# Attention and a gated MLP in one kernel, ordered by a written-out plan: groups 2 and 3 of the heads summed singly instead of as a pair, and a new order

## The chip, the cores and the metric

One core of a Trainium2 chip runs the whole program. The metric is the device time of one execution in microseconds (us). The engines are TensorE (PE in the profile, with its weight loads as PEld), VectorE (DVE), ScalarE (ACT), GpSimd (POOL) and SyncE (SP), which here only issues DMAs.

## The reference

There are 8 batches, 12 heads, 448 positions and 64 columns per head. The attention's output, laid out as 448 x 768 per batch, goes into a spatially gated MLP.

```python
q_n, k_n = rmsnorm(q, g_q), rmsnorm(k, g_k)            # over the 64 columns
attn = softmax(q_n @ k_n.T / sqrt(64));  x = attn @ v  # per batch and head
h = maximum(x @ w_in, 0)                               # 768 -> 1024
u, v = h[..., :512], h[..., 512:]
v_n = (v - mean(v)) / sqrt(var(v) + 1e-6)
out = (u * (w_spatial @ v_n + b_spatial)) @ w_out      # 512 -> 768, float32
```

## The kernel before

**Groups.** The 96 heads are 24 groups of four: group G belongs to batch G // 3. For each group, q and k are loaded (`op_L`, L287; i is 0 for q, 1 for k, 2 for v), squared (`op_Q`, on the engine that the plan names), summed over the 64 columns on VectorE (`op_R`), turned into a factor by a small log and exponential on ScalarE (`op_I`, `op_J`) and normalised (`op_N`, VectorE or GpSimd). They are transposed either by seven TensorE products (`op_P`) and a copy out of PSUM (`op_K`), or by a transposing DMA on SP's queue (`op_T`, L482; for k the scaled copy `op_Z` follows). V is cast to bf16 by `op_F`.

**Softmax.** A group has seven score blocks (`op_S`, L501): eight products of 64 rows by 32 columns of the array, each 448 long, into two PSUM banks. For group 0 a block (but the last) uses only the cells of one row half, each twice (`unit`, L494). ScalarE takes the exponential of a block into SBUF (`op_E`, L514, 168 in all). Then each of the seven columns of blocks is multiplied three times: with ones for the sum (`op_s`), and with the two halves of V (`op_a`, `op_b`). One such step for one group is here called a pass. It is four products, one per head, and the two heads of a pair lie in different row halves:

```python
for l in range(4):
    r, hh = divmod(l, 2)
    at = 64 * (hh ^ flip(G))
    ...
    pe.matmul(out=ps[32 * l:32 * l + 32, where[kind, G][0], 0:S], lhsT=w, rhs=et_of(G, r, c)[at:at + 64],
              start=(n == 1), stop=(n == C), tile_position=(at, 32 * l))
```

A pass takes four of the eight cells of 64 x 32. `flip` (L309) is 1 for the groups in the set `SECOND`; for those the two heads change row halves, and their V comes in by two loads of half the size, which `op_L` issues. A plan word `a.G.c.1` runs the pass of G and that of G + 1, a paired pass, which takes all eight cells; `a.G.c.0` runs that of G alone, a single pass. Before the change all groups are paired, (0, 1), (2, 3) and so on. `op_D` and `op_d` on ScalarE make the reciprocal of the sum by log and exponential, and `op_X` (L570, VectorE) scales a half of V's result into xt, the input of the MLP; there are two xt tiles, for even and for odd batches.

**MLP.** Per batch: V products (`op_V`, L589) for three row tiles, the fourth with the tail of the previous batch's output in `op_W` (L618), U products (`op_U`, L655), the statistics and normalisation (`op_c`, `op_B`, `op_M`, `op_m`, `op_A`), the spatial products (`op_H`, L669), the gate (`op_G`) and the output products (`op_O`, L683) with their copies and stores. The first of all is batch 0's first V product.

**Order.** All of it is issued in the order of the words in `PLAN`; each engine runs its share strictly in that order, and the framework adds waits for data and buffers. A word is `name.arguments/slots/engine`, with slots as base-36 digits (PSUM banks for S and the passes). Ten buffers hold loaded tiles, three hold squares, four normalised tiles, 22 exponentials. Operations of VectorE and GpSimd between SBUF tiles that share a port (`port`, L280) also wait for the other engine's last such operation. `op_z` (L249) issues idle products of 448 columns on TensorE, whose result is not used.

Of the kernel before, what the change touches and what calls it, by code (L numbers as in the profile page):

```python
# [19 lines left out]
SECOND = {1, 3, 5, 7, 9, 11, 13, 15, 17, 19, 21, 23}  # L20

PLAN = """
l.0.0/0/a l.1.0/1 gl.0//g l.0.1//a l.1.1 L.1.1/2 gl.1//g setup L.1.0/3 L.2.1/4 L.2.0/5 z.12/0 L.3.1/6 q.0.0/0/v
L.3.0/7 q.1.0/1/a r.0.0 wb/0 r.1.0 L.4.0/8 q.0.1//a L.5.0/9 q.1.1//a r.0.1 i.0//a r.1.1 j.0//a n.0.0//g i.1//a j.1//a
gA Q.1.1/2/a ws n.0.1//v p.0.0/0 L.1.2/0 R.1.1 n.1.0//g gB/1 Q.1.0/0/a p.0.1/2 n.1.1//g gC k.0.0/0/a p.1.0/1 R.1.0
Q.2.1/1/g L.4.1/1 k.0.1//a p.1.1/3 k.1.0/0/v I.1//a k.1.1//v S.0.0/01 J.1//a S.0.1/45 Q.2.0/2/a wi.0.1 N.1.1/0/v
S.0.6/23 E.0.1/0/a R.2.0 L.0.2/2 P.1.1/6 N.1.0/1/g E.0.6/1/a S.0.3/45 R.2.1 E.0.0/2/a S.0.2/23 Q.3.0/0/g
L.5.1/3 E.0.3/3/a K.1.1/1/v S.0.5/01 P.1.0/7 I.2//a E.0.2/4/a K.1.0/1/v wi.0.2 J.2//a E.0.5/5/a N.2.1/2/v
S.1.3/23 S.1.6/45 E.1.3/6/a N.2.0/3/v L.7.1/4 P.2.1/0 Q.3.1/2/a S.1.1/67 K.2.1/2/v L.6.0/5 S.1.5/12 Q.5.0/1/g
E.1.6/7/a P.2.0/3 R.3.1 E.1.5/8/a S.1.0/45 Y.0/0 R.3.0 Q.4.0/2/g E.1.1/9/a K.2.0/2/v E.1.0/a/a S.1.4/12 S.0.4/67 R.5.0  # L30
Y.2/3 I.3//a E.1.4/b/a Q.4.1/0/g y.0//v S.1.2/45 J.3//a y.2//v E.0.4/c/a S.2.6/01 S.2.3/23 E.2.6/d/a wx//g N.3.0/0/v
s.0.3.1/67 s.0.6.1 E.1.2/e/a S.2.1/01 F.1//v s.0.4.1 L.3.2/7 s.0.5.1 E.2.3/f/a R.4.0 s.0.2.1 N.3.1/1/g s.0.1.1
S.2.5/45 s.0.0.1 L.9.1/0 E.2.1/g/a P.3.0/2 R.4.1 E.2.5/h/a Q.5.1/1/v L.2.2/6 P.3.1/3 D.0/1/a I.4//a S.2.4/01
K.3.1/3/v Y.1/4 F.0//g E.2.4/i/a K.3.0/3/v J.4//a wi.0.3 L.6.1/2 D.1/0/a S.3.1/56 y.1//v b.0.5.1/01 wi.1.1 S.2.0/23
N.4.0/2/v E.3.1/j/a a.0.6.1/47 b.0.3.1 b.0.1.1 a.0.0.1 d.1//a b.0.0.1 S.3.0/56 L.7.0/8 E.2.0/k/a b.0.6.1 F.3//v
b.0.4.1 b.0.2.1 a.0.2.1 N.4.1/3/v a.0.3.1 L.8.1/7 E.3.0/l/a S.3.6/23 E.3.6/a/a X.1.1 S.3.3/56 Q.6.0/2/g R.5.1 P.4.0/1
d.0//a Y.3/2 K.4.0/0/v I.5//a E.3.3/1/a wi.1.0 P.4.1/3 F.2//v wi.0.0 J.5//a y.3//a N.5.1/0/v S.3.4/56 wi.1.3 a.0.5.1
a.0.4.1 E.3.4/7/a S.3.5/12 wi.1.2 a.0.1.1 K.4.1/0/v Q.6.1/0/g E.3.5/e/a s.2.0.1/56 X.0.1 s.2.4.1 s.2.1.1 s.2.3.1 X.0.0
Q.7.1/1/a s.2.6.1 s.2.5.1 S.2.2/01 S.3.2/23 N.5.0/1/g R.6.1 E.2.2/0/a P.5.1/4 E.3.2/c/a X.1.0 S.4.4/01 K.5.1/1/v
Q.9.1/0/g E.4.4/6/a T.5.0/1 b.2.5.1/72 s.2.2.1 R.6.0 b.2.4.1 a.2.1.1/34 D.2/1/a a.2.3.1 b.2.6.1 a.2.6.1 L.4.2/1 d.2//a  # L40
R.7.1 a.2.4.1 Q.7.0/2/g b.2.3.1 D.3/0/a L.5.2/6 b.2.0.1 S.4.6/01 b.2.1.1 I.6//a b.2.2.1 E.4.6/8/a a.2.0.1 a.2.2.1
X.2.1 L.8.0/3 S.4.1/56 Q.8.1/1/g a.2.5.1 d.3//a L.9.0/9 X.2.0 E.4.1/4/a V.0.0.0/7 X.3.1 V.0.0.1 J.6//a X.3.0 V.0.0.2
N.6.1/2/g R.7.0 S.4.5/56 c.0.0//a S.4.2/01 S.5.5/23 E.4.2/5/a V.0.2.1/4 R.8.1 V.0.1.0/7 N.6.0/3/g L.10.0/2 E.4.5/b/a
# [111 lines left out]
def kernel(  # L155
# [153 lines left out]
    def flip(G):  # L309
        return int(G in SECOND)  # L310

# [440 lines left out]
```

## Time and profile before

| | |
|---|---|
| median of 3 runs | 269.86 us (269.24 to 270.5) |
| the profiled execution | 270.1 us, span 268.3 us, mean granted TensorE clock 0.987 |
| TensorE / ScalarE / VectorE / GpSimd busy | 249.9 / 220.5 / 210.1 / 127.8 us |
| first V product of batch 0 | 46.98 us |
| DMA moved | 55.48 MB, mean 207 GB/s |

Times within the execution are microseconds from the span's start. Busy time is the union of an engine's instructions, and rows of TensorE, ScalarE and VectorE overlap a little because the engines are pipelined. In timeline rows the columns are start, length, engine, line, operation, tiles and count, and in brackets the idle time before with what ended it.

### The profile page before, as it was taken

Reading aid. Unit: us, or ns where it says so; the run is one execution under the profiler, and the core shown is the slowest. Engines: PE = TensorE matmul, PEld = TensorE weight load, DVE = VectorE, ACT = ScalarE, POOL = GpSimd, SP = SyncE. Lnnn points to the kernel's source line nnn. Section 1 sums busy time; section 2 is a strip of 40 time slices with the busy share of each in tenths; the row PEclk is TensorE's granted clock in tenths of the full one; section 3 lists DMA queues with packets and bytes.
Section 4 is the critical chain, followed back from the end, with each engine's and each line's share of the span. In section 5 each row is a group of like instructions: output and inputs, shape, how many; then the busy total and the mean of one; then the engine's idle time right before and its main releaser. Section 6 shows DMA issues by size and latency. Waiting matters only on the chain.

```text
span 268.3 us, 9975 instructions
## 1 busy us (share of the span) xinstructions
PE 249.9 (93%) x4296; PEld 128.0 (48%) x4296; DVE 210.1 (78%) x363; ACT 220.5 (82%) x363; POOL 127.8 (48%) x99
## 2 busy tenths in 40 slices
PE   5788786999999998999999999999999999999993
PEld 2434544445445554445545454454445546645551
DVE  5979998899889886899899989786868554457841
ACT  4999998899989998999989998999798976430532
POOL 2859569995465951656755358840464000000000
PEclk9968999999999999999999999999999999999999
DMA  7999899999999999999997999999374114110225
GB/s 248 366 268 330 237 256 153 313 250 288 189 220 254 323 226 306 283 284 244 199 288 175 259 220 250 308 136 173 131 166 121 61 61 149 74 45 2 88 116 209
DMA packets 58462, 55.48 MB, mean 207 GB/s; under 512 B 34609, under 2 KB 54130, under 8 KB 58418
## 3 DMA queue, kind: packets, MB, share of 16 engines
q1 hardware_dynamic: 56098, 51.52, 75.5%
q0 software_dynamic: 1952, 2.76, 5.8%
q8 instruction: 33, 0.54, 0.8%
q10 hardware_dynamic: 368, 0.56, 0.6%
q14 instruction: 11, 0.09, 0.1%
HBM read 38.55 MB, written 11.01 MB: 185 GB/s over the span
## 4 chain that ended last, share of the span: by engine, by line
PE 75%; DMA 10%; POOL 5%; issue 3%; DVE 2%; ACT 2%; SPq 0%; POOLq 0%; DVEq 0%
PE ps L544 15%; PE ps L655 13%; PE ps L683 11%; PE ps L589 11%; PE ps L509 11%; PE ps L669 8%; DMA raw<-in_k_dram 7%; PE ps L618 5%; POOL nrm L429 3%; DMA kr<-nrm 2%; DMA raw<-in_q_dram 1%; POOL sqt L385 1%; POOL nrm L437 1%; ACT et L517 1%; DVE os L366 1%
## 5 line engine op out<-in xcount | busy, mean ns | idle before, releaser
L517 ACT ACTIVATE et<-ps 128x896 bf16<-128x896 f32 x168 | 146.3, 922 | 11.3 <-PE ps L509 10.0
L429 POOL TENSOR_TENSOR nrm<-raw,rs 128x896 bf16<-128x896 f32 x37 | 62.0, 1687 | 42.0 <-ACT rs L414 34.0
L509 PE MATMUL ps<-qT,kT 64*32 64x448 bf16 x1344 | 57.5, 360 | 6.0 <-ACT et L517 2.0
L396 DVE TENSOR_REDUCE ss<-sqt 128x14 f32<-128x896 f32 x46 | 48.5, 1073 | 1.2 <-POOL sqt L385 1.2
L385 POOL TENSOR_TENSOR sqt<-raw 128x896 f32<-128x896 f32 x24 | 40.1, 1678 | 11.1 <-DVE nrm L429 4.7
L655 PE MATMUL ps<-xt,w_in 128*128 128x448 bf16 x192 | 43.2, 353 | 0.0
L544 PE MATMUL ps<-et,vt 64*32 64x448 bf16 x1344 | 41.5, 349 | 1.8 <-DVE xt L573 1.4
L589 PE MATMUL ps<-w_in,xt 128*128 128x512 bf16 x144 | 37.8, 380 | 0.0
L573 DVE TENSOR_TENSOR xt<-ps,rc 128x448 bf16<-128x448 f32 x48 | 27.7, 617 | 12.0 <-PE ps L544 7.5
L683 PE MATMUL ps<-w_out,gt 128*128 128x384 bf16 x192 | 36.2, 326 | 0.4 <-ACT et L517 0.4
L509 PEld LDWEIGHTS <-kT 64*32 64x32 bf16 x1344 | 20.3, 90 | 30.8 <-issue 21.7
L544 PEld LDWEIGHTS <-vt 64*32 64x32 bf16 x1344 | 21.8, 92 | 12.8 <-issue 3.4
L366 DVE COPY os<-ps 128x384 f32<-128x384 f32 (+1 forms) x32 | 17.5, 554 | 12.6 <-PE ps L683 7.5
L669 PE MATMUL ps<-w_spT,vn 128*128 128x448 bf16 (+1 forms) x128 | 27.3, 353 | 0.0
L655 PEld LDWEIGHTS <-w_in 128*128 128x128 bf16 x192 | 17.6, 98 | 20.1 <-issue 4.8
L683 PEld LDWEIGHTS <-gt 128*128 128x128 bf16 x192 | 17.7, 98 | 16.5 <-issue 4.3
L674 DVE TENSOR_TENSOR gt<-ps,us 128x448 bf16<-128x448 f32 x32 | 19.0, 619 | 7.3 <-PE ps L669 6.0
L544 PE MATMUL ps<-et,ones 64*32 64x448 bf16 x672 | 23.5, 350 | 0.6 <-ACT et L517 0.6
L320 POOL CAST vt<-raw 128x896 bf16<-128x896 f32 x16 | 14.8, 929 | 17.8 <-DVE sqt L385 8.6
L630 DVE BATCH_NORM_STATS2 s<-vs 128x6 f32<-128x512 bf16 (+1 forms) x32 | 21.7, 680 | 1.4 <-ACT vs L580 0.9
L364 ACT ACTIVATE os<-ps 128x384 f32<-128x384 f32 (+1 forms) x32 | 15.6, 490 | 6.2 <-PE ps L683 5.1
L589 PEld LDWEIGHTS <-xt 128*128 128x128 bf16 x144 | 12.7, 98 | 16.7 <-issue 5.2
(65 smaller groups left out, 262.5 us busy)
## 6 DMA issues: line engine op xcount, KB each, us to landing
raw<-in_k_dram SPq DMA_DIRECT2D x23, 448.0 KB, 6.0
raw<-in_q_dram SPq DMA_DIRECT2D x23, 448.0 KB, 6.3
out_dram<-os SPq DMA_DIRECT2D x24, 384.0 KB, 2.4
raw<-in_v_dram SPq DMA_DIRECT2D x24, 224.0 KB, 4.5
raw<-in_v_dram SPq DMA_DIRECT2D x12, 448.0 KB, 4.8
w_in<-in_moe_w_in_dram POOLq DMA_DIRECT2D x8, 192.0 KB, 7.1
out_dram<-os SPq DMA_DIRECT2D x7, 192.0 KB, 3.3
w_out<-in_moe_w_out_dram POOLq DMA_DIRECT2D x1, 768.0 KB, 9.2
```

Source lines behind the costliest of these rows:

```text
L385: port(eng, eng.tensor_tensor(out=t, in0=x, in1=x, op=ALU.mult))
L396: dve.tensor_reduce(out=sss[G % 3][:, i].rearrange("p r c -> p (r c)"), in_=sqt[where.pop(("sq", G, i))].rearrange("p r (c d) -> p (r c) d ...
L429: port(eng, eng.tensor_tensor(out=nrm[sl[0]].rearrange("p c r d -> p r c d"), in0=raw[where["raw", G, i]].rearrange("p r (c d) -> p r c d" ...
L509: pe.matmul(out=ps[at:at + 32, sl[n], 0:S], lhsT=kT[64 * r:64 * r + 64, c, 64 * hh + 32 * x:64 * hh + 32 * x + 32], rhs=qT[64 * r:64 * r + ...
L517: act.activation(out=ets[sl[0]].rearrange("q r (p c) -> q r p c", c=C), in_=ps[:, a:b + 1:b - a, 0:S].rearrange("q r (c p) -> q r p c", c= ...
L544: pe.matmul(out=ps[32 * l:32 * l + 32, where[kind, G][0], 0:S], lhsT=w, rhs=et_of(G, r, c)[at:at + 64], start=(n == 1), stop=(n == C), til ...
L573: dve.tensor_tensor(out=xts[b % 2][:, 2 * g + half, :], in0=ps[:, where.pop(("ab"[half], G))[0], 0:S], in1=rcs[where["rc", G]], op=ALU.mult)
L589: pe.matmul(out=ps[:, bank, :], lhsT=xts[b % 2][:, j, 128 * m:128 * m + 128], rhs=w_in[:, j % 2, j // 2, DH:], start=(n == 1 and j == 2 * ...
L630: dve.bn_stats(out=s6, in_=vss[b % SLOTS["vs"]][rows, m, :])
L655: pe.matmul(out=ps[:, bank, 0:S], lhsT=w_in[:, j % 2, j // 2, 128 * f:128 * f + 128], rhs=xts[b % 2][:, j, :], start=(n == 1 and j == 2 * ...
L669: pe.matmul(out=ps[:, sl[0], 0:S], lhsT=vns[b % SLOTS["vn"]][rows, m, 128 * f:128 * f + 128], rhs=w_spT[rows, m, :], start=(m == 0), stop= ...
L683: pe.matmul(out=ps[:, sl[0], 0:384], lhsT=gts[b % 2][:, f, 128 * m:128 * m + 128], rhs=w_out[:, f, 384 * h:384 * h + 384], start=(f == 0), ...
```

## The change

Group 3 leaves the set of flipped groups, the words of the passes of groups 2 and 3 become single (42 for 21), and the whole order is new: every line of `PLAN` differs. The engines of some words change, the idle products become 22 in four places (`z.11`, `z.5`, `z.4`, `z.2`, and `h.3`, three of 64 columns) instead of 12 in one, and group 1's q is transposed by a DMA (`T.1.0`) instead of by TensorE (`P.1.0`, `K.1.0`). The operations' functions are the same, one line further down.

```diff
-SECOND = {1, 3, 5, 7, 9, 11, 13, 15, 17, 19, 21, 23}
+SECOND = {1, 5, 7, 9, 11, 13, 15, 17, 19, 21, 23}
...
-Q.9.1/0/g E.4.4/6/a T.5.0/1 b.2.5.1/72 s.2.2.1 R.6.0 b.2.4.1 a.2.1.1/34 D.2/1/a a.2.3.1 b.2.6.1 a.2.6.1 L.4.2/1 d.2//a
...
+E.3.0/l/a S.3.1/12 a.2.2.0/0 wi.1.0 Q.7.1/1/v s.2.0.0 E.3.1/6/a b.2.5.0/4 S.3.3/56 wi.0.1 s.2.2.0 b.2.1.0 E.3.3/a/a
```

On SP's queue, near the start of the program (raw is a loaded tile, rc is borrowed for the bias): before, q and k of groups 2 and 3, then of 4 and 5, follow each other without a wait on an engine's result but for free buffers.

```order
L292 DMA raw_69<-in_q_dram 128x2x448
L292 DMA raw_70<-in_k_dram 128x2x448
L292 DMA raw_71<-in_q_dram 128x2x448
L338 DMA rc_113<-in_moe_b_spatial_dram 1x448
L292 DMA raw_72<-in_q_dram 128x2x448
L292 DMA raw_73<-in_q_dram 128x2x448
L297 DMA raw_64<-in_v_dram 64x2x448 x2
L292 DMA raw_65<-in_k_dram 128x2x448
```

The same place now:

```order
L339 DMA rc_113<-in_moe_b_spatial_dram 1x448
L293 DMA raw_69<-in_k_dram 128x2x448
L293 DMA raw_70<-in_q_dram 128x2x448
L293 DMA raw_71<-in_k_dram 128x2x448
L485 DMA_TRANSPOSE qT_82<-nrm_77 128x7x128
L293 DMA raw_72<-in_q_dram 128x2x448
L293 DMA raw_73<-in_q_dram 128x2x448
L293 DMA raw_64<-in_v_dram 128x2x448
```

The transposing DMA of group 1's q has moved in ahead of the loads of groups 4 and 5 (raw_72, raw_73), and it waits for nrm_77, the normalised tile.

On VectorE, around the scaling that ends batch 0's attention (xt_131 is the tile of batch 0 and 2, xt_132 that of batch 1; ss is a row sum, kT a scaled copy, vs the copy of the first V products' result). Before:

```order
L396 TENSOR_REDUCE ss_115<-sqt_74 128x14
L573 TENSOR_TENSOR xt_131<-ps,rc_113 128x448
L467 TENSOR_SCALAR kT_88<-ps,g_col 128x896
L396 TENSOR_REDUCE ss_115<-sqt_76 128x14
L396 TENSOR_REDUCE ss_116<-sqt_75 128x14
L573 TENSOR_TENSOR xt_131<-ps,rc_114 128x448 x2
L573 TENSOR_TENSOR xt_132<-ps,rc_113 128x448 x2
L396 TENSOR_REDUCE ss_116<-sqt_76 128x14
L396 TENSOR_REDUCE ss_117<-sqt_75 128x14
L582 TENSOR_SCALAR vs_133<-ps 128x512
```

Now:

```order
L397 TENSOR_REDUCE ss_116<-sqt_75 128x14
L397 TENSOR_REDUCE ss_115<-sqt_76 128x14
L574 TENSOR_TENSOR xt_131<-ps,rc_113 128x448 x2
L397 TENSOR_REDUCE ss_115<-sqt_74 128x14
L397 TENSOR_REDUCE ss_116<-sqt_75 128x14
L386 TENSOR_TENSOR sqt_76<-raw_71 128x896
L430 TENSOR_TENSOR nrm_79<-raw_68,rs_121 128x2x7x64
L397 TENSOR_REDUCE ss_117<-sqt_76 128x14
L583 TENSOR_SCALAR vs_133<-ps 128x512
L574 TENSOR_TENSOR xt_132<-ps,rc_114 128x448 x2
```

Group 2's two scalings (the last of batch 0) have moved apart from group 3's, which now follow the first copy of a V product's result instead of standing ahead of it.

249 lines of the change are left out of this document (125 added, 124 removed).

## The prediction

> **What bounds the kernel now.** I read the totals and the slices of the page first, then the stretches that the trace gives by window, then the two ends of TensorE's own timeline.
>
> ```profile
> PE 249.9 (93%) x4296; PEld 128.0 (48%) x4296; DVE 210.1 (78%) x363; ACT 220.5 (82%) x363; POOL 127.8 (48%) x99
> PE   5788786999999998999999999999999999999993
> ACT  4999998899989998999989998999798976430532
> ```
> ```profile
> 0.00:12.90 12.90, 8.50 (x66) 4.41 (x66) 9.55 (x21) 8.73 (x16) 7.71 (x14) 1.00 0.90 308
> 12.90:46.98 34.08, 26.60 (x672) 14.82 (x672) 30.51 (x41) 32.53 (x51) 25.44 (x21) 0.90 1.00 249
> 46.98:264.05 217.07, 214.80 (x3561) 108.75 (x3558) 169.48 (x302) 178.80 (x297) 94.70 (x65) 1.00 0.81 195
> 36.20:46.98 10.78, 7.82 (x262) 4.76 (x259) 8.98 (x14) 9.97 (x17) 9.42 (x9) 1.00 1.06 206
> ```
> ```profile
> 46.98 1.47 PE L589 MATMUL ps<-w_in,xt 128*128 128x512 bf16 x6
> 263.16 0.84 PE L618 MATMUL ps<-w_out,gt 128*64 128x384 bf16 x8
> ```
>
> The columns of the windows are length, then busy time of TensorE, its weight loads, VectorE, ScalarE and GpSimd, then granted clock, DMA share and GB/s. The kernel has two stages with different limits. From 46.98 us, where the first product of batch 0's MLP starts, to 264.05 TensorE is busy 214.80 of 217.07 us: it is the bound, with 2.27 us idle. Before that, from the first exponential at about 12.9, ScalarE is busy 32.53 of 34.08 us and TensorE only 26.60, so ScalarE leads and TensorE has 7.48 us to spare, 2.96 of it (10.78 less 7.82) in the last 10.78 us. So I ask two questions: **when does the first MLP product start in the new order, and how much TensorE work is then left?** What lies around the span (270.1 for the profiled execution against 268.3) I leave as it is.
>
> **The change part by part.** *Work left after that start.* Counted in the plan, both orders issue every pass of groups 0 to 3 ahead of the first MLP product. The old one has 31 score blocks ahead of it and the new one 33, so 135 are left instead of 137. All else that TensorE does later has the same count, and it goes from small tiles to full products 49 times in both. A block costs 0.19 to 0.25 (rows below), so two are about 0.46 us less work left.
>
> *Passes.* A paired pass puts eight products into eight cells of the array, a single one four into four.
>
> ```profile
> 62.44 1.32 PE ps L544 x56
> ...
> 44.98 0.19 PE ps L509 x8
> ```
> ```profile
> 13.95 0.56 PE L509 MATMUL ps<-qT,kT 64*32 64x448 bf16 x8
> ...
> 34.08 0.38 PE L509 MATMUL ps<-qT,kT 64*32 64x448 bf16 x8
> 36.03 0.57 PE L448 MATMUL ps<-ident,nrm 128*128 128x128 bf16 x7
> ```
>
> In the chain of waits seven paired passes take 1.32 us, 0.189 each, and a score block among passes 0.19. No single pass is in this trace. The nearest rows are group 0's score blocks: they use only four cells, each twice, and eight products take 0.56 from first start to last end where a block over eight cells takes 0.38. The difference, 0.18, is one more round through four cells; so I price a single pass at a full round, 0.189. Bounds: it can't be below half of that, 0.095, since half the products are in it; and twice 0.189 if four products did not run side by side. I take 0.189, the row it is nearest to. Groups 2 and 3 had 21 paired passes and now have 42 single ones: **+21 x 0.189 = +4.0 us** on TensorE. With ten more idle products (22 for 12, at 0.19: +1.9), the two score blocks (+0.4) and one set of seven transposes less (P.1.0, 0.57 in the row with its latency, about 0.5), TensorE has some 5.8 us more before its first MLP product. Sixteen of the 22 idle products come ahead of the first exponentials, where the engine waits for inputs; the others fall into its spare time. The cover for all this is the 7.48 us; where it is gone, each microsecond goes to the end.
>
> The Trainium skill (TensorE: Matmul & The Clock Gate, "Part 3: Packing small matmuls — row/col tiling") speaks against single passes: it says that a weight load overlaps running products only where its row group differs, and a single pass comes back to the same cells. By it and the row below every one of 42 passes could show a load of 0.092, +3.9 us more; the group-0 blocks above return to their cells too and show no load, so this trace is against it.
>
> ```profile
> L544 PEld LDWEIGHTS <-vt 64*32 64x32 bf16 x1344 | 21.8, 92 | 12.8 <-issue 3.4 <-POOL vt L320 0.4
> ```
>
> *ScalarE's bound on the start.* What the first MLP product stands behind is a score block (S.4.1) whose banks the 31st exponential frees; in the old order the 31st is the one that starts at 46.51.
>
> ```profile
> 12.89 3.35 ACT L517 ACTIVATE et<-ps 128x896 bf16<-128x896 f32 x4
> ...
> 29.38 0.64 ACT L563 ACTIVATE rc<-ps 128x448 f32<-128x448 f32 x1
> ...
> 32.65 0.57 ACT L567 ACTIVATE rc<-rc 128x448 f32<-128x448 f32 x1
> 33.12 2.52 ACT L517 ACTIVATE et<-ps 128x896 bf16<-128x896 f32 x3
> ...
> 37.09 0.54 ACT L364 ACTIVATE w_spT<-ps 64x448 bf16<-64x448 bf16 x1
> ...
> 39.22 0.95 ACT L383 ACTIVATE sqt<-raw 128x896 f32<-128x896 f32 x1
> ...
> 46.51 0.91 ACT L517 ACTIVATE et<-ps 128x896 bf16<-128x896 f32 x1
> ```
>
> Up to the 31st exponential the new order has two squares more on ScalarE (+1.9) and one qT copy (-0.9), one w_spT copy (-0.54), one log (-0.64) and one reciprocal (-0.57) less: about -0.8. If ScalarE lost none of its 1.55 us of idle time either, the 31st would end at 46.51 + 0.91 - 0.8 - 1.55 = 45.1, and with one block (0.38 with latency) the product could start at **45.5**.
>
> *TensorE's bound.* Block S.3.1 needs the banks that the 21st exponential frees. In the old order the 21st is the first of the three at 33.12 and ends at 34.0. The new order has moved ScalarE work ahead of it: three squares, one reciprocal and one each of the small log and exponential more, one qT copy less, about 2.5 us with the 0.1 by which rows on ScalarE overlap. So it ends at 36.5, and from there TensorE has 38 single passes and 11 score blocks to the first MLP product: 49 x 0.19 = 9.3, **45.8** at the earliest. The two bounds nearly meet, so neither engine covers the other's waits. In the old order the same stretch held 2.96 us of idle TensorE; the longest piece was this:
>
> ```profile
> 39.53 1.66 POOL sqt L385
> 41.21 1.09 DVE ss L396
> 42.30 0.54 DVE xt L573
> ```
> ```profile
> 42.88 0.38 PE L544 MATMUL ps<-et,vt 64*32 64x448 bf16 x8 [1.36 <-DVE xt L573]
> ```
>
> A column-scaling (xt) stood on VectorE behind a row sum that waited for GpSimd's square. The new order has fewer normalisations (4 for 7) and casts (1 for 3) on VectorE up to that point, and still has four row sums and a square in the queue around X.2. I take 2.0 us of waits, between none and the 2.96 of before, nearer to what was seen: the start is then at 47.8. **Sum:** 47.8 - 46.98 = +0.8 later, 0.46 less work left, later idle time as before (bounds: 2.27 less and as much more): +0.4, so 270.5 for an execution like the profiled one. That one, 270.1, lay 0.2 above the median of the runs shown, 269.86; I forecast a median of **270.3**.
>
> That batch 0 is finished ahead of group 3 earns nothing by itself here: its last xt columns no longer wait for group 3's passes, but in the new order the first MLP product stands on TensorE behind the last of those passes all the same.
>
> *Clock.* Idle products are there for the clock.
>
> ```profile
> 14.00:15.00 1.00, 0.84 (x17) 0.19 (x17) 1.00 (x2) 1.00 (x2) 1.00 (x1) 1.00 1.18 282
> 15.00:16.00 1.00, 0.76 (x16) 0.14 (x7) 0.97 (x2) 1.00 (x2) 1.00 (x2) 0.67 1.14 282
> ...
> 21.00:22.00 1.00, 1.00 (x15) 0.52 (x12) 1.00 (x2) 1.00 (x3) 0.96 (x2) 0.50 1.11 341
> 22.00:23.00 1.00, 1.00 (x34) 0.67 (x30) 1.00 (x2) 1.00 (x3) 1.00 (x1) 0.92 1.09 256
> ```
>
> ```profile
> 13.45 0.56 PE L448 MATMUL ps<-ident,nrm 128*128 128x128 bf16 x7 [0.79 <-DVE nrm L429]
> ```
> ```profile
> 18.64 0.92 ACT L517 ACTIVATE et<-ps 128x896 bf16<-128x896 f32 x1 [0.48 <-PE ps L509]
> ```
>
> The granted clock is half from about 15.3 to 22.1, and some 6 us of work in it take twice their time, 3 us. ScalarE waited for TensorE only 0.48 us there, so those 3 us are part of the spare time, and their return is worth between nothing and 0.5; I take nothing. I expect them back, since five idle products now stand among the first transposes. The Trainium skill (same page, "Part 4: PE-mode transpose") says that transposes don't count as work for the clock gate; that the clock fell after a stretch of transposes from 8.1 to 11.3 agrees, as the longest idle piece between 8 and 15 was 0.79 us.
>
> **The rivals.** *The start comes at its bound (faster).* For it: VectorE and GpSimd have less to do up to the start, and the clock is whole. Then the start is at 45.8, 1.2 earlier, with 0.46 less left, and if the later idle time halves too (1.1) the sum is -2.8: a median of 267.1, and up to 268.5 with part of it. Against it: the two engines then work at 100% side by side for ten microseconds, which they do nowhere in the front of this trace. Chance 0.22.
>
> *Single passes bind (slower).* Place: TensorE from S.3.1 to the first MLP product. Each block there waits for an exponential two blocks back, each exponential for its block, and three to four single passes (0.57 to 0.76) stand between blocks where an exponential takes 0.8. If the waits stay at 2.96 and ScalarE's returns add about one more, the start is at 49.8: +2.8 - 0.46 = +2.3, 272.2. It decides from about 48.8 on, where the time passes the half per cent. Chance 0.18.
>
> *The transposing DMA is late (slower).* Group 1's q now goes through a transposing DMA instead of TensorE, on SP's queue, with all later loads behind it.
>
> ```profile
> DMA to landing us min/median/max: 2.9/4.6/8.1
> ```
> ```profile
> 13.49 1.68 POOL L429 TENSOR_TENSOR nrm<-raw,rs 128x896 bf16<-128x896 f32 x1 [0.62 <-DVE nrm L429]
> ```
> ```profile
> 10.67 0.38 SPq L292 DMA_DIRECT2D raw<-in_k_dram  x1
> ```
>
> Its normalisation ran second on GpSimd, at 13.49, and is now first, ending by about 13.5 (estimate from these rows); the transpose lands at 18.1, or 21.6 with the longest time. It is wanted after six exponentials and a square, at 12.9 + 6 x 0.81 (from the row of four at 12.89) + 1.2 = 19.0. The load of 10.67 (group 4's k) waits until 15 or so; group 3's V, no longer halved, is one load for two and changes nothing. At the median nothing happens; at the maximum ScalarE stands for 2.6 us, and ScalarE leads there: up to 272.9. Chance 0.12.
>
> **How the numbers follow.** Forecast 0.48, faster 0.22, single passes 0.18, late transpose 0.12. The range leaves out the far ends of the faster case and of the two slower ones and the unlikely price of shown weight loads: 267.9 to 273.0. A measurement of this kernel can tell about 0.5% (1.35 us) from no change: faster 0.22, same 0.48, slower 0.30.
>
> **What would show it.** First MLP product near 47.8 (45.8: faster rival; over 48.8: a slower one); seven single passes at 1.32 in the chain; granted clock 1.0 from 15 to 22 with nothing gained by it; ScalarE without a gap ahead of the seventh exponential; about 216.6 us from the first MLP product to the last matmul. I am wrong if that last stretch changes by over 2 us, for then the new order matters after the front, where I gave it nothing, or if the first exponential moves by more than 0.5.

## The result and the profile after

The changed kernel is slower: 279.1 us median (277.12 to 280.62, 4 runs) against 270.18 (269.24 to 271.29, 4 runs), a ratio of 1.0335, 95% interval 1.0287 to 1.0382. A later set of five rounds (e15) gave 278.31 and 1.0273 (1.0230 to 1.0316). The forecast was 270.3, no change. The profiled execution took 277.12 us with a span of 275.3, so 7.0 of the 8.9 us between the medians are to be found between it and the one of before.

The totals of the changed kernel's page:

```profile
PE 259.3 (94%) x4302; PEld 131.6 (48%) x4302; DVE 210.7 (77%) x362; ACT 221.0 (80%) x364; POOL 124.8 (45%) x98
```

ScalarE and VectorE have as much to do as before, GpSimd 3 us less, and TensorE is busy 9.4 us more. The totals don't say where that comes from. The same three stretches as in the prediction do, cut at the changed kernel's own first exponential, first MLP product and last matmul (columns as there):

```profile
0.00:14.98 14.98, 10.53 (x55) 5.14 (x59) 10.05 (x20) 8.66 (x15) 8.78 (x15) 1.00 0.87 272
14.98:49.86 34.88, 31.83 (x709) 18.44 (x702) 28.25 (x39) 32.92 (x51) 25.58 (x23) 1.00 0.97 249
49.86:270.84 220.98, 216.92 (x3546) 107.98 (x3542) 171.80 (x304) 178.91 (x298) 90.45 (x61) 1.00 0.79 191
39.80:49.86 10.06, 9.86 (x247) 6.31 (x245) 8.97 (x12) 9.84 (x15) 6.77 (x7) 1.00 0.99 180
```

TensorE's 9.4 us are 7.3 ahead of the first MLP product (42.36 for 35.10), where the prediction had 5.8, and 2.1 behind it, where it had 0.46 less. The first exponential comes 2.1 us later (14.98 for 12.89), the first MLP product 2.9 later (49.86 for 46.98), and the **late stretch** from there to the last matmul takes 220.98 us for 217.02, though two score blocks less are in it. So some 3 us are lost ahead of the first MLP product and 4 behind it. In the late stretch TensorE's idle time rose from 2.3 to 4.1 us, and its busy time from 214.80 to 216.92, which can't be work: products of the same shapes are counted in longer rows.

**Ahead of the first exponential.** VectorE first, then ScalarE, then TensorE (timeline columns as in the prediction):

```profile
7.08 1.15 DVE L403 TENSOR_REDUCE ss<-sqt 128x7 f32<-128x448 f32 x2 [0.95 <-POOL sqt L386]
8.14 1.66 DVE L371 SCALAR_TENSOR_TENSOR g_row<-g_row 1x128 f32<-1x128 f32 x1
9.73 2.06 DVE L397 TENSOR_REDUCE ss<-sqt 128x14 f32<-128x896 f32 x2
```
```profile
11.82 0.32 ACT L410 ACTIVATE ls<-ss,eps 128x28 f32<-128x28 f32 x1 [1.11 <-DVE ss L397]
...
14.98 0.92 ACT L518 ACTIVATE et<-ps 128x896 bf16<-128x896 f32 x1 [0.90 <-PE ps L510]
...
19.61 0.92 ACT L518 ACTIVATE et<-ps 128x896 bf16<-128x896 f32 x1 [0.93 <-PE ps L510]
20.97 2.54 ACT L518 ACTIVATE et<-ps 128x896 bf16<-128x896 f32 x3 [0.45 <-PE ps L510]
```
```profile
8.81 0.95 PE L457 MATMUL ps<-ident,nrm 128*64 128x128 bf16 x7 [1.20 <-POOL nrm L438]
...
11.25 2.05 PE L253 MATMUL ps<-ident 128*128 128x448 bf16 x5
13.23 2.43 PE L510 MATMUL ps<-qT,kT 64*32 64x448 bf16 x24
...
17.23 1.68 PE L253 MATMUL ps<-ident 128*128 128x448 bf16 x4
...
19.47 0.56 PE L449 MATMUL ps<-ident,nrm 128*128 128x128 bf16 x7
```

TensorE in the kernel before, for the rate of the same transposes:

```profile
9.09 0.58 PE L456 MATMUL ps<-ident,nrm 128*64 128x128 bf16 x7
```

The row sums of group 0's second half wait for a square that is now on GpSimd, the row of g follows, and the sums for group 1 start at 9.73 (8.75 before), so ScalarE stands 1.11 us. Then TensorE runs at half rate, seven transposes in 0.95 instead of 0.58, up to about 19.4, and ScalarE waits for its blocks 0.90, 0.93 and 0.45 us.

**Late.** The longest row in the list of TensorE's waits behind the first MLP product (us in sum, times, longest), and the longest of the list of before, which has no wait of a block for an exponential:

```profile
PE ps L510 <- ACT et L518: 2.1, 5, 0.9
```
```profile
PE ps L509 <- issue: 1.2, 1, 1.2
```

L510 are the score blocks (L509 before), which wait for an exponential to free their banks; "issue" is a stand of TensorE for nothing that the profile names, on which the last section has more. TensorE's rows of the changed kernel with these waits:

```profile
134.88 0.38 PE L510 MATMUL ps<-qT,kT 64*32 64x448 bf16 x6 [0.16 <-ACT et L518]
...
142.09 0.38 PE L510 MATMUL ps<-qT,kT 64*32 64x448 bf16 x6 [0.90 <-ACT et L518]
...
146.83 0.38 PE L510 MATMUL ps<-qT,kT 64*32 64x448 bf16 x8 [0.29 <-ACT et L518]
...
207.27 0.38 PE L510 MATMUL ps<-qT,kT 64*32 64x448 bf16 x6 [0.31 <-ACT et L518]
...
216.02 0.38 PE L510 MATMUL ps<-qT,kT 64*32 64x448 bf16 x8 [0.42 <-ACT et L518]
```

Each row can be found in the plan. At 142.09 it is block S.15.2 in banks 4 and 5. Bank 5 was used by S.12.6, and between the two stands one block, S.14.5, which is 0.24 us of TensorE's work, while the exponential that frees the bank takes 0.92. The other four are S.13.4, S.14.4, S.21.6 and S.23.6. For every late block I added up the TensorE work between it and the block whose exponential freed its banks (a block 0.24, a pass 0.19, a V, U, O or H word 0.44, 0.38, 0.65 and 0.76). In the order of before no block has less than 1.13 us. In the new one six have 1.0 or less: 0.24 (S.13.4, S.15.2), 0.57 (S.21.6), 0.62 (S.23.6), 0.81 (S.14.4) and 1.00 (S.21.4). Five of these six are the five rows above. The distance doesn't set the wait alone: S.13.4 and S.15.2 have the same 0.24 and show 0.16 and 0.90. Part of a wait can also stand inside a busy row: a row of x6 is the rest of a block whose first two products had gone ahead.

Some executions are disturbed and take a per cent or two longer, the profiled ones of e4 and e11 among them: of these two profiles only the front and the waits are used, and the ratios below leave such executions out, which the medians don't.

### The profile page after: what moved, and what is told of

It is laid out like the page before. It is cut to its first block, busy times and chain, and to the rows that moved or that the text cites. A ratio compares the mean times of both kernels' runs of the same rounds, so it can differ in the third digit from the quotient of the medians.

```text
span 275.3 us, 9984 instructions
## 1 busy us (share of the span) xinstructions
PE 259.3 (94%) x4302; PEld 131.6 (48%) x4302; DVE 210.7 (77%) x362; ACT 221.0 (80%) x364; POOL 124.8 (45%) x98
## 4 chain that ended last, share of the span: by engine, by line
PE 74%; ACT 8%; issue 5%; POOL 4%; DVE 3%; DMA 3%; POOLq 0%; ACTq 0%; DVEq 0%
PE ps L545 15%; PE ps L656 12%; PE ps L510 12%; PE ps L684 12%; PE ps L590 10%; PE ps L670 9%; ACT et L518 6%; PE ps L619 3%; DMA raw<-in_q_dram 3%; POOL sqt L386 2%; PE ps L253 1%; PE ps L457 1%; DVE nrm L430 1%; POOL nrm L430 1%; DVE g_row L371 1%
## 5 line engine op out<-in xcount | busy, mean ns | idle before, releaser
L430 POOL TENSOR_TENSOR nrm<-raw,rs 128x896 bf16<-128x896 f32 x35 | 58.8, 1688 | 21.1 <-DVE nrm L430 9.0
L510 PE MATMUL ps<-qT,kT 64*32 64x448 bf16 x1344 | 61.9, 358 | 3.8 <-ACT et L518 3.1
L386 POOL TENSOR_TENSOR sqt<-raw 128x896 f32<-128x896 f32 (+1 forms) x25 | 41.1, 1649 | 32.5 <-DMA raw<-in_q_dram 8.3
L545 PE MATMUL ps<-et,vt 64*32 64x448 bf16 x1344 | 48.2, 350 | 2.3 <-issue 1.6
L510 PEld LDWEIGHTS <-kT 64*32 64x32 bf16 x1344 | 22.6, 90 | 32.8 <-issue 24.1
L545 PEld LDWEIGHTS <-vt 64*32 64x32 bf16 x1344 | 22.7, 92 | 16.3 <-issue 5.6
L545 PE MATMUL ps<-et,ones 64*32 64x448 bf16 x672 | 26.7, 350 | 0.3 <-ACT et L518 0.2
L367 DVE COPY os<-ps 128x384 f32<-128x384 f32 (+1 forms) x30 | 16.2, 551 | 14.0 <-PE ps L684 5.4
L365 ACT ACTIVATE os<-ps 128x384 f32<-128x384 f32 (+1 forms) x34 | 16.6, 494 | 11.1 <-PE ps L684 8.6
```

The source lines that it names most:

```text
L386: port(eng, eng.tensor_tensor(out=t, in0=x, in1=x, op=ALU.mult))
L430: port(eng, eng.tensor_tensor(out=nrm[sl[0]].rearrange("p c r d -> p r c d"), in0=raw[where["raw", G, i]].rearrange("p r (c d) -> p r c d" ...
L510: pe.matmul(out=ps[at:at + 32, sl[n], 0:S], lhsT=kT[64 * r:64 * r + 64, c, 64 * hh + 32 * x:64 * hh + 32 * x + 32], rhs=qT[64 * r:64 * r + ...
```

## The experiments

Line numbers differ by one or two between kernels, with the number of lines of the plan. The stages of all profiled executions, in us, one execution each; the ratio is to the kernel before on the same chip:

| kernel | first exponential | first MLP product | late stretch | median | ratio, 95% interval |
|---|---|---|---|---|---|
| before | 12.89 | 46.98 | 217.0 | 270.18 | |
| changed | 14.98 | 49.86 | 221.0 | 279.1 | 1.0335 (1.0287 to 1.0382) |
| e1 | 12.72 | 48.57 | 216.7 | 271.27 | 1.0015 (0.9978 to 1.0052) |
| e2 | 14.32 | 54.20 | 220.4 | 279.28 | 1.0303 (1.0244 to 1.0361) |
| e3 | 14.87 | 49.69 | 221.8 | 278.13 | 1.0253 (1.0202 to 1.0304) |
| e4 | 14.13 | 50.17 | | 280.77 | 1.0259 (1.0146 to 1.0371) |
| e5 | 12.79 | 50.84 | 322.7 | 376.97 | 1.3998 (1.3890 to 1.4106) |
| e6 | 14.89 | 51.95 | 225.5 | 284.91 | 1.0550 (1.0456 to 1.0643) |
| e7 | 13.85 | 48.74 | 223.2 | 276.85 | 1.0255 (1.0169 to 1.0341) |
| e8 | 13.48 | 51.92 | 224.7 | 283.76 | 1.0521 (1.0430 to 1.0613) |
| e9 | 12.72 | 46.43 | 216.4 | 269.57 | 0.9966 (0.9923 to 1.0009) |
| e10 | 14.99 | 52.43 | 217.0 | 275.91 | 1.0226 (1.0164 to 1.0289) |
| e11 | 14.27 | | | 277.0 | 1.0171 (1.0089 to 1.0254) |
| e12 | 13.52 | 48.92 | 219.4 | 276.7 | 1.0245 (1.0190 to 1.0300) |
| e13 | 14.22 | 47.37 | 216.5 | 271.24 | 1.0021 (0.9990 to 1.0053) |
| e14 | 12.62 | 48.65 | 221.4 | 275.39 | 1.0163 (1.0126 to 1.0200) |
| e15 | 14.97 | 50.42 | 222.4 | 278.31 | 1.0273 (1.0230 to 1.0316) |

### e1: single passes in the kernel before

```diff
-SECOND = {1, 3, 5, 7, 9, ...}
+SECOND = {1, 5, 7, 9, ...}
```

> The old order word for word, with group 3 out of the flipped set: the words of the passes stay paired, but the eight products of a step of groups 2 and 3 now share four cells, so they cost TensorE two rounds (+21 x 0.189 = 4.0 us), and the V of group 3 is one load instead of two. Theory P (the single passes show in the time because the spare time of the front is not there to take them): first MLP product 1 to 4 us after 46.98, ratio 1.004 to 1.015. Theory C (the half clock and the idle products of the new front are the cause): below 0.5 us, ratio 1.000 to 1.002. Theory L (the new order's later part is the cause): as C. From the first MLP product to the last matmul all expect 217 within 0.7.

The paired words of groups 2 and 3 then need two rounds through the same cells, as the single ones do. In the profile the first MLP product is 1.6 us later; in time nothing is seen, and 0.5% is the most that the interval leaves. In this order the single passes don't cost 8 us. What they cost in the changed order, where TensorE is busy 9.86 of the last 10.06 us ahead of the first MLP product, this run doesn't say.

### e2: group 3 flipped again in the changed kernel

```diff
-SECOND = {1, 5, 7, 9, ...}
+SECOND = {1, 3, 5, 7, 9, ...}
```

> The new order word for word, with group 3 back in the flipped set, so that single passes of groups 2 and 3 that stand next to each other can share the array. P: the nine microseconds of passes before the first MLP product shrink by 1 to 2, first MLP product at 48 to 49 instead of 49.86, ratio to the kernel before 1.027 to 1.031. C and L: no change beyond 0.5 us, 1.030 to 1.036. From the first MLP product to the last matmul all expect 221 within 1.

No gain in time. In this execution the load of group 3's V, now in two halves, lands later, and the front waits for it; GpSimd, VectorE, TensorE:

```profile
43.27 0.92 POOL L321 CAST vt<-raw 128x896 bf16<-128x896 f32 x1 [5.25 <-DMA raw<-in_v_dram]
```
```profile
44.23 1.09 DVE L386 TENSOR_TENSOR sqt<-raw 128x896 f32<-128x896 f32 x1 [4.75 <-POOL vt L321]
45.24 0.68 DVE L468 TENSOR_SCALAR kT<-ps,g_col 128x896 bf16<-128x896 bf16 x1
```
```profile
45.97 0.59 PE L545 MATMUL ps<-et,vt 64*32 64x448 bf16 x8 [3.98 <-DVE kT L468]
```

The load holds GpSimd's cast, the cast holds a square on VectorE (`port` puts the one behind the other), the square holds the copy of a kT behind it, and that copy frees the bank that the first pass of group 3 takes. In the changed kernel the cast ends at 39.95, in time. That the halves are the reason isn't shown: in e4, with one whole load, the cast waits too and ends at 41.47. With this wait in it, the run doesn't tell what passes that share the array would have gained.

### e3 and e4: the idle products

```diff
e3:  -z.11/0 h.3 ... z.5/3 ... z.4/2 ... z.2/7     +z.11/0
e4:  -z.11/0 h.3                                   +z.20/0
```

> The new order without the 11 idle products in the three later places and without the three short ones. C: the five and four that ran at half speed (2.05 and 1.68 us) no longer stand ahead of the score blocks, so the first exponential comes at 13.5 to 14.3 instead of 14.98 and the first MLP product 1 to 2 us earlier than 49.86, unless the clock stays half beyond 20 us, which would take it back; ratio 1.026 to 1.030. P: the first MLP product moves by less than 0.7, as the stretch of passes sets it, 1.031 to 1.036. L: 221 us from the first MLP product on, as in the new order.

> The new order with 20 idle products at the very start (for 11 and three short ones), which fill the time before the first transposes. C: the clock is whole when the transposes come: seven of them take 0.57 as in the old kernel's first 12 us and not 0.95, the first exponential comes 1.5 to 2 us earlier than 14.98, the first MLP product 1.5 to 3 us earlier, ratio 1.023 to 1.029. P and L: within 0.7 us of the new order, 1.031 to 1.036; from the first MLP product on 221.

Without the idle products behind the first eleven, front and late stretch are as they were: they cost nothing that these runs can tell. With twenty at the start TensorE's first transposes take 0.58 us each set and the first exponential comes 0.85 earlier, at 14.13. In e2 and e11, whose words are the changed kernel's up to there, the first transposes took 0.58 too, and the first exponential came at 14.32 and 14.27. So 0.7 to 0.85 of the 2.1 us at the first exponential is TensorE's rate. What that buys by itself isn't shown: in e4's profile the first MLP product comes no earlier, as TensorE waits at the first pass of group 3, as in e2, and the ratio's interval is wide (1.0146 to 1.0371).

```profile
43.25 0.37 PE L545 MATMUL ps<-et,vt 64*32 64x448 bf16 x4 [1.84 <-DVE kT L468]
```

### e5, e6 and e8: the two orders crossed

e5 has all words of before up to the first MLP product and then the changed order's, e6 the reverse. Both needed other slots at the seam.

> All words of the order up to the first MLP product stand as in the kernel before; everything behind it stands in the order of the changed kernel (groups 2 and 3 paired as before, since their passes lie ahead of that product; ten buffer slots near the seam are another one of the same kind, because the two orders hold different ones there). Theory L (the order behind the first MLP product costs some 4 us by itself): first MLP product at 47.0 as before, 220 to 221.5 us from it to the last matmul, median 274 (1.013 to 1.018 of before). Rival F (the late stretch only suffers from what the changed front hands over: later loads and casts, another set of live buffers): 216.5 to 217.5 us behind the first MLP product, median 270 to 270.8 (0.998 to 1.003).

> The other half: all words up to the first MLP product as in the changed kernel, everything behind it in the order of the kernel before (some loads near the seam stand a little later, where their buffer comes free). Theory L: first MLP product at 49.9, then 216.5 to 217.5 us, median 273 (1.009 to 1.013). Rival F: 220 to 221.5 us behind the first MLP product, median 277 (1.025 to 1.03). If both halves are slow in the late stretch, it is the seam of the two and neither theory is told apart.

e5 was of no use for its question, since I had renumbered PSUM banks without thinking of the blocks: a block's exponential reads two banks as one strided tile, and with the banks apart it waited for other work. ScalarE's longest such row:

```profile
57.28 0.92 ACT L517 ACTIVATE et<-ps 128x896 bf16<-128x896 f32 x1 [6.18 <-DVE xt L573]
```

This exponential (E.5.5) reads banks 1 and 7, and the scaling (X.3.1) read bank 2. That the framework takes the banks in between as read too is my reading of rows like this one. e8 keeps the two banks of every block side by side:

> Again the front of the kernel before with the changed kernel's order behind it, now with the two PSUM banks of every score block side by side, as in both kernels (in the first try 117 of 168 blocks had banks apart). From batch 1's last V product (the W word of batch 1, at 74.3 in the changed kernel, 196.5 us ahead of its last matmul) all work is the same as in the changed kernel, so that stretch is the test, free of the seam. Theory L (the order behind the first MLP product costs some 4 us by itself): 196 to 198 us there, and a median of 274 to 276 if the seam costs nothing. Rival F (the late stretch only suffers from what the changed front hands over): 191.5 to 193.5 us there, median 270 to 272.

In both, loads and blocks were out of place at the seam: from the first MLP product to batch 1's tail product (its last V product) e8 takes 28.9 us where the changed kernel takes 24.4, and e6 39.5 where before takes 29.5. Behind it is the test. TensorE's rows of that product and of the last matmul, for the changed kernel, e8, before and e6:

```profile
74.27 0.40 PE L619 MATMUL ps<-w_in,xt 128*64 128x512 bf16 x1
```
```profile
80.86 0.40 PE L618 MATMUL ps<-w_in,xt 128*64 128x512 bf16 x1
...
275.82 0.84 PE L618 MATMUL ps<-w_out,gt 128*64 128x384 bf16 x8
```
```profile
76.46 0.40 PE L618 MATMUL ps<-w_in,xt 128*64 128x512 bf16 x1
```
```profile
91.49 0.40 PE L619 MATMUL ps<-w_in,xt 128*64 128x512 bf16 x1
...
276.56 0.84 PE L619 MATMUL ps<-w_out,gt 128*64 128x384 bf16 x8
```

From the first row to the end of the last, the changed order takes 196.6 us behind its own front (270.84 - 74.27) and 195.8 behind that of before; the old order takes 187.5 behind its own and 185.9 behind the changed one. (The two can't be compared with each other here, since different work is left at that product.) So each order keeps its late time, within 1.6 us, whatever front it follows, where rival F has a change of 4: the late loss is made by the words behind the first MLP product. Rival F falls, for this part of the late stretch; the words between the first MLP product and the tail product weren't tested.

### e7: the front mended in three places

```diff
-... z.11/0 h.3 ... q.0.0/0/a ... q.0.1//g ... L.6.0/6 ... L.3.2/5
+... z.20/0     ... q.0.0/0/v ... q.0.1//a ... L.3.2/6 ... L.6.0/5
```

> The changed kernel with its front mended in three places: twenty idle products in one piece instead of fourteen; the two squares of group 0's q on VectorE and ScalarE as before instead of ScalarE and GpSimd; the load of group 3's V takes the place (and buffer) of the load of group 6's q, which takes that of the V. Theory of two causes ahead of the first MLP product (late row sums of group 0, then the late load of group 3's V): first exponential at 12.9 to 13.3, first MLP product at 47.3 to 48.3, late stretch as in the changed kernel (220.5 to 222), median 274.5 to 276 (1.017 to 1.022). Rival (ScalarE's work itself sets the first MLP product): first exponential earlier but the first MLP product still at 49.5 or later, median 277 or more (1.025 up).

The first exponential came at 13.85 and the first MLP product at 48.74, both 1.1 earlier, between the two theories: a stand of TensorE of 1.35 us without a wait on record is part of it. The late stretch was 2.2 longer, with another such stand of 2.1, so the time shows little of the gain.

### e9 and e10: half of every late exponential left out

```diff
+        n = 64 if G < 4 else 32
-        act.activation(out=ets[...]..., in_=ps[...]..., ...)
+        act.activation(out=ets[...]...[:, :, 0:n], in_=ps[...]...[:, :, 0:n], ...)
```

> The kernel before with half of each exponential left out from group 4 on (32 of 64 query positions of each chunk; the other half of those buffers keeps old values), TensorE's work unchanged. Theory C (TensorE's late waits are score blocks that wait for an exponential): the late stretch falls from 217.0 to 214 to 215.5, since 2.27 us of idle time and some hidden waits are all there is to win; median 267 to 269. Rival M (they are something else): 216.5 to 217.5, median 270.

> The changed kernel with half of each exponential left out from group 4 on, as in the run beside it. Theory C: the late stretch falls from 221.0 to 213.5 to 216, within 1 us of the other's, and the difference of the two medians shrinks from 7 to 9 us to 3 to 4 (the front's). Rival M: it stays at 220 to 221.5, 4 us above the other's, median 276.5 to 278.

The late stretches of e9 and of e10, in the windows of the trace:

```profile
46.43:262.86 216.43, 212.96 (x3545) 107.07 (x3558) 169.39 (x303) 132.44 (x297) 95.00 (x65) 1.00 0.80 195
```
```profile
52.43:269.41 216.98, 214.54 (x3531) 106.29 (x3542) 171.45 (x304) 133.24 (x297) 90.55 (x61) 1.00 0.79 193
```

With ScalarE 46 us less busy, the order of before gains 0.6 us and the changed one 4.0; 0.55 us of the late difference is left. Stands of TensorE blur this. Without them (1.15 us in before, 1.08 in the changed kernel, 1.81 in e9, 0.85 in e10) the difference goes from 4.0 to 1.5. So **most of the late loss, some 2.5 of 4.0 us, is waiting for ScalarE**. Whether single places do it or a queue that is behind as a whole, these two runs can't say, since both are relieved. The lower busy times say nothing here: both traces lack 15 or 16 products, all of them V products, whose rows of the changed kernel and of e10 are these:

```profile
L590 PE MATMUL ps<-w_in,xt 128*128 128x512 bf16 x144 | 37.3, 380 | 0.0
```
```profile
L591 PE MATMUL ps<-w_in,xt 128*128 128x512 bf16 x129 | 35.5, 380 | 0.7 <-issue 0.2
```

The late busy times of blocks and passes, added up, hardly fall (98.3 us in before and 100.9 in the changed kernel, 97.8 in e9 and 100.8 in e10), so what is left of the difference is to be looked for there. The medians still differ by 6.3 us, where 3 to 4 were expected, as e10's first MLP product came 6.0 us behind e9's: its front lost 2.6 us against the changed kernel's, of which 2.3 are a stand at 39.7.

### e11 and e12: six blocks moved, then the front mended as well

```diff
-S.13.4/56 O.2.2.1/0 Z.15/2/v T.17.1/0 R.19.1 U.3.1.2 o.2.2.1/4/a
+O.2.2.1/0 Z.15/2/v T.17.1/0 R.19.1 U.3.1.2 S.13.4/56 o.2.2.1/4/a
...
-L.1.1/2 l.1.1                          (e12 alone, with e7's edits)
+l.1.1 L.1.1/2
```

The other five are moved in the same way, past one or two of TensorE's words (S.15.2 with its exponential), and S.21.0, which would have come too close, past one pass.

> The changed kernel with the score blocks moved that stand closest behind the block whose PSUM banks they take over: six late blocks have less than 1.0 us of TensorE work between the two (0.24, 0.24, 0.57, 0.62, 0.81, 1.00), where the exponential that frees the banks takes 0.92; no late block of the kernel before has less than 1.13. They go past two to four of TensorE's next words, to 0.95 to 1.65. Theory B (these places are the loss): TensorE's waits for an exponential behind the first MLP product fall from 2.1 us (5 times) to under 0.7, the late stretch from 221.0 to 218.3 to 219.5, median 2 us below the changed kernel's (1.022 to 1.027 of before). Rival Q (ScalarE's queue is behind as a whole, so blocks wait wherever they stand): waits at other places, late stretch 220.4 to 221.5, median as the changed kernel's (1.03 to 1.035).

> The same six blocks moved, and the front mended as in the third kernel of the run before last, with one thing more: the load of the second half of group 0's k ahead of the load of group 1's k, as in the kernel before (the changed kernel has them the other way round, and its square waited for that load). Theory (first exponential sets the first MLP product 34.9 us later, and the late places cost 2): first exponential at 12.9 to 13.4, first MLP product at 47.7 to 48.4, late stretch 218.3 to 219.5, median 273 to 274.5 (1.009 to 1.015). Rival Q for the late part: late stretch 220.4 or more and a median of 275 to 276.5 (1.018 to 1.024).

The waits of score blocks for an exponential are gone in both lists. e12's windows and its list of TensorE's late waits:

```profile
13.52:48.92 35.40, 29.96 (x705) 18.91 (x702) 29.31 (x40) 33.06 (x52) 27.60 (x24) 1.00 1.00 255
48.92:268.29 219.37, 216.47 (x3545) 107.53 (x3542) 171.97 (x304) 178.49 (x298) 90.44 (x61) 1.00 0.78 192
```
```profile
PE ps L590 <- issue: 1.9, 1, 1.9
PE ps L545 <- ACT et L518: 0.2, 1, 0.2
PE ps L545 <- ACT us L581: 0.2, 1, 0.2
PE ps L670 <- ACT et L518: 0.2, 1, 0.2
```

The late stretch is 219.4, as theory B has it, with a stand of 1.9 us in it. Without the stands it is 2.5 us shorter than the changed kernel's (217.4 for 219.9), which is what halving the exponentials gave, and 1.6 longer than that of before. The profiled execution took 274.58 us. The times are less clear: e11 came out 1.7% above before and e12 2.4%, with intervals that overlap that of the changed kernel (e15), and e12's median is 2 us above its profiled execution. So the six places' worth is shown in the trace and not in the time; what the other executions of e12 lose has no trace.

### e13, e14 and e15: each suspect alone in the kernel before, and the changed kernel again

```diff
e13  -... l.1.1 L.1.1/2 ... q.0.0/0/v ... q.0.1//a
     +... L.1.1/2 l.1.1 ... q.0.0/0/a ... q.0.1//g
e14  -E.13.1/k/a O.2.0.0/4 X.11.1 L.19.0/0 O.2.2.1/0 E.12.2/l/a o.2.0.0/2/v X.10.0 S.12.4/12
     +E.13.1/k/a S.12.4/12 O.2.0.0/4 X.11.1 L.19.0/0 O.2.2.1/0 E.12.2/l/a o.2.0.0/2/v X.10.0
```

e14 moves S.9.0, S.16.2, S.19.6, S.20.4 and S.22.4 in the same way.

> The kernel before with three things of the changed front alone: the load of the second half of group 0's k stands behind the load of group 1's k, group 0's first q square runs on ScalarE instead of VectorE and its second on GpSimd instead of ScalarE. Theory D (the first exponential sets the first MLP product; ScalarE's work from there is the same): first exponential 1.0 to 2.1 us later (13.9 to 15.0), first MLP product later by as much within 0.7, late stretch as before (216.5 to 217.5), median 1 to 2 us above the kernel before (1.004 to 1.008). Rival (the delay is taken up in ScalarE's two us of idle time on the way): first MLP product at 46.5 to 47.5 and no change (0.998 to 1.002).

> The kernel before with six late score blocks put directly behind the exponential's place in the order that frees their banks: 0.24 to 0.38 us of TensorE work now stand between the block that used the banks and the one that takes them over, 1.24 to 1.6 before. Everything else, banks too, stays. Theory B (a block that takes over banks sooner than an exponential can free them holds TensorE): waits of blocks for an exponential at six places, 1.5 to 3.5 us in sum, the late stretch from 217.0 to 218.8 to 220.5, median 1.007 to 1.013 of before. Rival Q (ScalarE's queue as a whole decides): the blocks wait but the time comes back at their old places, late stretch within 0.7 us of before, median 0.998 to 1.003.

> The changed kernel itself once more, for the spread of its stages from run to run and beside the two others: first exponential 14.8 to 15.1, first MLP product 49.5 to 50.5, late stretch 220 to 222, waits of score blocks for an exponential 1.8 to 2.3 us, median 277 to 279.5 (1.026 to 1.034).

**e14 settles the late part.** TensorE's six rows, and the late window:

```profile
98.69 0.57 PE L508 MATMUL ps<-qT,kT 64*32 64x448 bf16 x16 [0.61 <-ACT et L516]
...
132.76 0.38 PE L508 MATMUL ps<-qT,kT 64*32 64x448 bf16 x8 [0.85 <-ACT et L516]
...
164.19 0.38 PE L508 MATMUL ps<-qT,kT 64*32 64x448 bf16 x8 [0.67 <-ACT et L516]
...
186.76 0.38 PE L508 MATMUL ps<-qT,kT 64*32 64x448 bf16 x8 [0.66 <-ACT et L516]
...
198.14 0.38 PE L508 MATMUL ps<-qT,kT 64*32 64x448 bf16 x8 [0.85 <-ACT et L516]
...
218.96 0.38 PE L508 MATMUL ps<-qT,kT 64*32 64x448 bf16 x8 [0.67 <-ACT et L516]
```
```profile
48.65:270.08 221.43, 215.54 (x3561) 109.03 (x3558) 169.41 (x302) 178.65 (x297) 94.87 (x65) 1.00 0.79 191
```

Six words put earlier by about a microsecond of work make six waits, 4.31 us in sum, and a late stretch 4.4 us longer; nothing of it is given back. The median rises by 1.63%, more than I expected. So single places are enough for such a loss. e15, the changed kernel again, has its first exponential at 14.97, its first MLP product at 50.42 and 1.9 us of waits of blocks for exponentials at four places; its late stretch, 222.4, lies a little above what was expected.

**e13 went against me.** The first exponential came 1.3 us later, the first MLP product only 0.4, and the time didn't change. Its window from the first exponential to the first MLP product, and ScalarE's only waits in it:

```profile
14.22:47.37 33.15, 27.80 (x677) 16.11 (x673) 30.21 (x41) 32.38 (x51) 25.57 (x21) 0.85 0.97 243
```
```profile
19.97 0.92 ACT L516 ACTIVATE et<-ps 128x896 bf16<-128x896 f32 x1 [0.48 <-PE ps L508]
...
33.17 0.92 ACT L516 ACTIVATE et<-ps 128x896 bf16<-128x896 f32 x1 [0.25 <-PE ps L508]
```

The kernel before has the same two waits and a third of 0.78 at 43.49, ahead of a logarithm; e13 lacks that one, so the delay is taken up there. The changed order has no such slack: its waits lie mostly early (0.93 and 0.45 at 20 us, 0.35 and 0.22 at 39 and 42), and from 39.80 on TensorE is busy 9.86 of 10.06 us and ScalarE 9.84.

## Why the prediction was wrong, point by point

1. **Two stages, ScalarE ahead of the first MLP product and TensorE behind it:** right as a reading of the profile. It misled in one respect: that TensorE is busy 99% of the late stretch was taken to mean that ScalarE doesn't matter there. ScalarE sets when banks come free, and e10 beside e9 shows some 2.5 us of it.

2. **"later idle time as before (bounds: 2.27 less and as much more)": this step failed, and with it the forecast.** The new order behind the first MLP product costs 4.0 us; it was counted by its work alone (-0.46). e8 and e6 show that the late time belongs to those words, e9 and e10 that some 2.5 us of it are waiting for ScalarE, e14 that blocks that take over banks too soon make such a loss by themselves, 0.6 to 0.85 us a place. In the changed kernel five such places show 2.1 us of waits, and with them moved (e12) the late stretch without its stands is 2.5 us shorter. The other 1.5 us lie in longer busy rows of blocks and passes, and no run shows why. The bounds failed for a reason: they were made from the idle time that was there, while a wait depends on the distance of two words in the new order, which could have been counted from the plan. Of the 7.0 us this step is 4 and the start of point 4 most of the rest.

3. **A single pass at 0.189, +4.0 us:** right. Between 39.80 and 49.86 stand 38 single passes and 11 blocks in 10.06 us, 9.3 by the price. The Trainium skill (TensorE: Matmul & The Clock Gate, "Part 3: Packing small matmuls — row/col tiling") says that a weight load overlaps running products only in another row group. By that the loads of passes that return to the same cells would show; at 0.2 us of idle time in these 10 us the trace is against it, as the prediction held. The ten more idle products were mis-sized: at 0.19 each they were to cost 1.9, but most ran at half rate, and the 22 took 8.6 us (4.29, 2.05, 1.68 and 0.55) where the 12 had taken 4.66.

4. **ScalarE's bound, 45.5, and TensorE's, 45.8:** the chain behind the 21st exponential was priced rightly, but its start was not. The 21st ended at 39.8, not 36.5. Of these 3.3 us, 2.1 are the first exponential, which the sum had silently left at 12.89, and most of the rest ScalarE's waits for TensorE on the way (0.93, 0.45 and 0.35, where before had 0.48 and 0.25).

5. **2.0 us of waits, start at 47.8:** the waits were 0.2 where I had put them; the start came at 49.86 for another reason, the late start of the chain in point 4. What the single passes cost there in time isn't shown; 38 of them and 11 blocks kept TensorE busy for all but 0.2 us. The faster rival counted on less work for GpSimd too; up to the first MLP product it was busy 34.4 us, for 33.2 before. The argument against that rival, that the two engines "work at 100% side by side ... which they do nowhere in the front", was refuted: here they do. The rival that came near in time, single passes that bind (49.8), had the wrong mechanism: it needed 4 us of waits.

6. **Clock, worth nothing to 0.5, "I expect them back":** wrong. TensorE ran at half rate from 8.8 to 19.4, where the kernel before had it from 15.3 to 22.1, and the first exponential lost 0.7 to 0.85 us by it (e2, e4, e11). The rest of its 2.1 us lies in the front's order: loads, squares and the row of g. e7 and e12, which undo parts of these, bring it to 13.85 and 13.52. Which share each has isn't settled; alone in the kernel before they cost nothing in time (e13).

7. **The transposing DMA:** right; ScalarE's waits in the front name score blocks, and none stands ahead of the seventh exponential.

8. **What would show it wrong:** both signs that were named came: a first exponential moved by over 0.5, and a late stretch changed by over 2 us.

What stays open: e12 has both causes undone in part and is still 2.4% above before by its median. Its late busy time is 1.7 us above that of before (216.47 for 214.80), with two blocks less of work, and no run shows what stretches these rows. TensorE's stands differ from execution to execution. None of the versions that do all of the work beats the kernel before.

## What to carry to other kernels

When an order is exchanged for another, don't price it by its work alone: for each buffer that is handed over, count the work that stands between its last user and its next on the engine that must not stop, and compare it with the time of the operation that frees it. Here 1.13 us was enough for an exponential of 0.92 in the order of before, 0.95 and 1.00 showed no wait in e12, and 0.24 to 0.81 was not enough. And state the starting point of a sum, here the first exponential, as a term of its own, to be derived from the new order like the others.

## What the runs showed of the hardware

**Half rate with a whole clock on record.** In the changed kernel's profiled execution the granted clock reads 1.00 throughout, while products of the same shape take nearly twice their time up to 19.4 us (0.95 for 0.58, rows above). In e15 the rate was the same from 10.4 us on, and there the record says 0.82 for the first stretch. The durations are the better witness. The Trainium skill (TensorE: Matmul & The Clock Gate, "Part 1: The HAM clock gate (the "warmup" mystery)") says that the full clock comes after a busy window of about 3.4 us that runs freely, so that it varies when the rate rises. The traces agree that it varies: the same fourteen idle products (3.16 to 7.61, 4.45 us) left the rate at half here and were followed by two sets of transposes at 0.58 in e11; 3.9 us of them gave the full rate for one set of transposes in e15, and 5.8 us held it in e4.

**TensorE stands for its instructions.** In the middle of a pass its weight loads and products stop together, and the profile names nothing that they wait for. TensorE's rows of the changed kernel, of e7 and of e10:

```profile
38.25 0.37 PE L545 MATMUL ps<-et,vt 64*32 64x448 bf16 x3 [0.93 <-issue]
```
```profile
36.84 0.36 PE L545 MATMUL ps<-et,ones 64*32 64x448 bf16 x1 [1.35 <-issue]
```
```profile
39.73 0.44 PE L546 MATMUL ps<-et,vt 64*32 64x448 bf16 x3 [2.29 <-issue]
```

It comes near 37 to 40 us in the changed front, where the DMA engines are busy all the time, and near 104 to 109 us in most kernels (1.15 in before, up to 2.3 in others), 0.2 to 2.6 us at a time. Its place is fixed in TensorE's own instructions and not in time: 479 products and 479 or 480 weight loads stand ahead of the first one in every trace that has it, and the next ones follow 256, 512 and about 2,550 instructions later (44.20 us in e6, 46.69 in before, 103.58 in before and 107.07 in the changed kernel). The DMA records fit: a queue that the profile calls an instruction queue moves 33 transfers of 16,384 bytes in an execution, for some 8,600 products and weight loads, so one for about 256. All 38 stands of 0.3 us or more in these seventeen traces, from 14 us on, end 1.2 to 1.8 us behind the end of such a transfer: the third one for the first place, the thirteenth for the one past 103 us. In the changed kernel, e7 and e10 the third ends at 36.80, 35.26 and 38.14 and the stand at 38.25, 36.84 and 39.73. So TensorE stands there for late instructions. What delays the transfers isn't tested. The stands are about as large as what several of these experiments were to tell apart, which is why the stages were read beside the times.
